# A softmax cut into seven pieces, work at the border of two steps moved ahead of the last groups of the second layer, and small products ordered by PSUM bank

## The chip, the cores and the metric

The kernel runs on one core of one Trainium2 chip. The metric is the device time of one execution in microseconds (us); the median of three runs before the change is 2174.5 us. TensorE is called PE here, VectorE DVE, ScalarE ACT, SyncE SP; these are the profile's names.

## The reference

For each of four batches, columns of q and k are normalised over the 6080 rows, a 256x256 score matrix goes through a softmax, and v is multiplied by it. The result goes through a two-layer network with a GELU between the layers.

```python
def _attn_ref(q, k, v, tau):             # q, k, v: (4, 6080, 256)
    qn = q / (np.linalg.norm(q, axis=1, keepdims=True) + 1e-06)
    kn = k / (np.linalg.norm(k, axis=1, keepdims=True) + 1e-06)
    s = kn.transpose(0, 2, 1) @ qn / tau
    s = s - s.max(-1, keepdims=True)
    a = np.exp(s)
    a /= a.sum(-1, keepdims=True) + 1e-09
    return (v @ a).astype(np.float32)

def _moe_ref(x, w_in, w_out):            # x: (24320, 256), w_in: (256, 2048), w_out: (2048, 256)
    h = x @ w_in
    g = 0.5 * h * (1.0 + erf(h * inv_sqrt2))
    return (g @ w_out).astype(np.float32)
```

## The kernel before

The softmax matrix of a batch is multiplied into `w_in` (`w_part`), so that the bulk of the work is two products: v times those weights (first layer), and the GELU of it times `w_out` (second layer). Numbers are split into a high and a low part (`vh`/`vl`, `wh`/`wl`, `gh`/`gl`), and a product takes three matmuls (`passes`): high by high, high by low, low by high.

**Steps.** A step is one `(b, p, u)`: batch b of 4, pair p of 6 (two chunks of 512 tokens, 480 in the last pair), unit u of 8 (two blocks of 128 hidden features). The 192 steps are counted by `i = (b*6+p)*8+u`. In a step, `first_products` makes the first layer of unit u by a Strassen scheme of seven products, called here **P0 to P6**, of three matmuls each. P0, P2, P4 and P6 go into one PSUM bank (`one`), P1, P3 and P5 into another (`two`). P0 and P1 are copied out by ACT (`p1`, `p5`), P2 too (`u2`). After P3, P4 and P5 DVE adds such a copy to the bank's contents (`added`), and ACT takes the GELU of the sum; the GELU of P6 is read by ACT straight from `one`. Where the unit's second layer is done by Strassen too (`mine`: most units with u > 0 from step 16 on), the GELUs of P5 and P6 go into `x`, and `sums` builds differences of its blocks on DVE and the high and low parts of all blocks on ACT and DVE (tiles `gh1`/`gl1`: called `hb`, `lb` in the code; `gh0`/`gl0`: `ht`, `lt`).

**The second layer lags a step.** Between the seven products of step i stand the groups of `second_products` of step i-1: one group of three matmuls after each of P0 to P3, one or two after P4 and P5, and what is left after P6. With Strassen these are four groups of width 512 and then seven small ones of width 256 (`work`), into the banks c00, c01, p0 and p1; three small ones are left after P6. Without it there are eight groups of 512, and two are left.

**Two banks in turn.** `bank()` hands out the two PSUM banks h0 and h1 in turn. P0 of a step takes the front bank of the ring, and at the end of `first_products` the bank of P6 is put at the back (`later`). So whatever takes a bank at the border of two steps gets the bank of P5 (`two`). If it does, P0 of the next step uses the bank that ACT's GELU of P6 reads, and P1 the bank of the border work. If nothing takes a bank there, P0 uses the bank of P5, and P1 that of P6.

**Work at the border.** Three kinds of work of the next batch take a bank: `burst` (eight matmuls for the scores of batch b, evicted by DVE into `sacc`), `w_part` (six matmuls of the softmax by `w_in`, evicted by ACT into a tile `hl`), and two steps of `softmax`: a product with `diag` that spreads the norms over all partitions (DVE reads it), and the four transposes of the exponentials (ACT reads them as `eh`, DVE as `el`).

**What sets the order.** Instructions run on each engine in the order in which the code issues them (`InOrder`). Work of the next batch is put into slots by `at(step, slot, job)`: slots 0 to 5 follow P0 to P5, slot 6 stands after the left-over groups of the second layer, `EDGE` (8) after `sums` has begun. `softmax(False)` is a generator that is resumed by `spread(gen, step, 12, 10 + EDGE, ...)`: 12 is slot 2 of the next step. With `base` the first step of batch b-1, the softmax of batch b stands in steps base+36 to base+38, `w_part` in base+41 to base+48, and the bursts in pairs of steps before.

Of the kernel before, what the change touches and what calls it, by code (L numbers as in the profile page):

```python
# [23 lines left out]
NCT = C // P  # L24
# [41 lines left out]
def channel_attention_gelu_ffn(ctx, tc, qk, kqt, vt, tau, w_in, w_out, out):  # L66
# [274 lines left out]
    def softmax(first):  # L341

        small = pm.tile([P, 32], F32, name="small")
        x, y, z, r = (small[:, 4 * i:4 * i + 4] for i in range(4))
        rk, nms, dens = (small[:, 16 + 2 * i:18 + 2 * i] for i in range(3))
        ts = []
        for m in range(NCT):
            t = pm.tile([P, C], F32, name=f"t{m}")
            if first:
                act.copy(out=t, in_=state["s"][m])  # L350
            else:
                s = state["sacc"]
                dve.tensor_tensor(out=t, in0=s[:, m, 0:C], in1=s[:, m, C:2 * C], op=ALU.add)
            ts.append(t)
        nsum = state.pop("nsum")
        if first:
            nps, acc = psum("c01"), state.pop("acc")
            with behind("scores"):
                for j in range(JS):
                    sum_up(nps, acc[:, j], j == 0, j == JS - 1)  # L360
            dve.reduce_sum(out=z, in_=nsum[:, :, NSQ // NSJ:NSC], axis=AX.X)
            dve.tensor_tensor(out=x, in0=nps[:, 0:2 * NCT], in1=z, op=ALU.add)
        else:
            dve.reduce_sum(out=x, in_=nsum[:, :, 0:NSC], axis=AX.X)
        dve.tensor_scalar(out=x, in0=x, scalar1=1e-30, scalar2=None, op0=ALU.max)
        yield

        if first:
            act.activation(out=y, in_=x, func=AF.Sqrt)
            preload(AF.Exp, y)  # L370
        else:
            dve.tensor_scalar(out=y.bitcast(I32), in0=x.bitcast(I32), scalar1=0.5, scalar2=float(ROOT),
                              op0=ALU.mult, op1=ALU.add)
            for part in (1.0, 0.25):
                dve.reciprocal(out=z, in_=y)
                dve.tensor_tensor(out=z, in0=z, in1=x, op=ALU.mult)
                dve.scalar_tensor_tensor(out=y, in0=y, scalar=part, in1=z, op0=ALU.mult, op1=ALU.add)
        dve.reciprocal(out=z, in_=y)
        dve.tensor_tensor(out=z, in0=z, in1=x, op=ALU.mult)
        dve.scalar_tensor_tensor(out=z, in0=z, scalar=2e-6, in1=y, op0=ALU.add, op1=ALU.add)  # L380
        dve.reciprocal(out=r, in_=z)

        diag = pm.tile([P, NCT, P], F32, name="diag")
        dve.tensor_tensor(out=diag, in0=ident.unsqueeze(1).broadcast_to([P, NCT, P]),
                                in1=r[:, NCT:2 * NCT].unsqueeze(2).broadcast_to([P, NCT, P]), op=ALU.mult)
        dve.tensor_scalar(out=rk, in0=r[:, 0:NCT], scalar1=rtau, scalar2=4.0, op0=ALU.mult, op1=ALU.mult)
        yield
        rq = psum("c10") if first else bank()
        mm(rq[:, 0:C], ones, diag.rearrange("p h d -> p (h d)"), start=True, stop=True)
        for m in range(NCT):  # L390
            dve.scalar_tensor_tensor(out=ts[m], in0=ts[m], scalar=rk[:, m:m + 1], in1=rq[:, 0:C],
                                           op0=ALU.mult, op1=ALU.mult)
            dve.reduce_max(out=nms[:, m:m + 1], in_=ts[m], axis=AX.X, negate=True)
        yield
        es = []
        rden = pm.tile([P, 8], F32, name="rden", bufs=2)
        for m in range(NCT):
            e = ts[m]
            den = dens[:, m:m + 1]
            act.activation(out=e, in_=ts[m], func=AF.Exp, bias=nms[:, m:m + 1], accum_out=den)  # L400
            es.append(e)
        if not first:
            yield
        for m in range(NCT):
            den = dens[:, m:m + 1]
            dve.tensor_scalar(out=den, in0=den, scalar1=1e-9, scalar2=None, op0=ALU.add)
            dve.reciprocal(out=rden[:, m:m + 1], in_=den)
        yield
        tp = psum("c11") if first else bank()
        tpv = tp.rearrange("p (d c) -> p d c", d=NCT)  # L410
        for m in range(NCT):
            for d in range(NCT):
                pe.transpose(out=tpv[:, d, m * P:(m + 1) * P], in_=es[m][:, d * P:(d + 1) * P],
                   identity=ident)
        eh = pm.tile([P, NCT, C], F32R, name="eh")
        el = pm.tile([P, NCT, C], F32R, name="el")
        marks["eh"] = act.copy(out=eh, in_=tpv)
        if first:
            preload(AF.Gelu, eh[:, 0, 0:2])
        marks["el"] = dve.tensor_tensor(out=el, in0=tpv, in1=f32(eh), op=ALU.subtract)  # L420
        state["e"], state["rden"] = (eh, el), rden
# [266 lines left out]
    def second_products(b, p, u, blocks):  # L688
# [14 lines left out]
        def wpair(c, i):  # L703
            cs = slice(c * P, (c + 1) * P)
            return wo[:, 0, i, cs], wo[:, 1, i, cs]
# [20 lines left out]
        if not mine:  # L726
            end = u == NU - 1
            for x in range(2 * NCT):
                c, i = divmod(x, NCT) if end and mixed else (x % NCT, x // NCT)
# [9 lines left out]
        ws = wss.pop((b, p, u))  # L739
        (hb, lb), (ht, lt) = blocks["b"], blocks["t"]  # L740
        last = not any(strassen(b, p, x) for x in range(u + 1, NU))
        work = (("c00", 1, wpair(0, 0), hb, lb, 2), ("p0", 0, wpair(0, 1), hb, lb, 0),
                ("c00", 0, (ws[:, 0, 3], ws[:, 1, 3]), hb, lb, 1), ("p1", 0, (ws[:, 0, 0], ws[:, 1, 0]), ht, lt, 0),
                ("p1", 1, (ws[:, 0, 2], ws[:, 1, 2]), ht, lt, 1), ("p0", 1, (ws[:, 0, 1], ws[:, 1, 1]), ht, lt, 2),
                ("c01", 1, wpair(1, 0), ht, lt, 3))
        for name, half, w, hi, lo, k in work:
            o, first = acc(name)
# [164 lines left out]
    FIRSTB = FILL // NB  # L912
    bursts = {}
    for b in range(1, B):
        start, num, den = (8, 5, 2) if b == 1 else (4, 14, 5)
        for k in range(FIRSTB if b == 1 else 0, NQS // NB):
            bursts[b, k] = (b - 1) * NP * NU + start + k * num // den

# [2 lines left out]
    def at(step, slot, job):  # L921
        jobs.setdefault((step, slot), []).append(job)

    def run(step, slot):
        for job in jobs.pop((step, slot), ()):
            job()

    def spread(gen, step, *slots):
        for x in slots:
            at(step + x // 10, x % 10, lambda: next(gen, None))  # L930

    EDGE = 8

    for (b, k), s in bursts.items():
        prev = bursts.get((b, k - 1), s - 3)
        for t in range(NB):
            js = k * NB + t
            at(prev - 1 + t, EDGE, lambda b=b, js=js: load_qk(b, js))

            def split(b=b, js=js, step=prev + 1 + t):  # L940
                gen = split_qk(b, js)
                next(gen)
                at(step, 2, lambda: next(gen, None))
            at(prev + 1 + t, 1, split)
        for m in range(NCT):
            at(s + m, EDGE, lambda b=b, k=k, m=m: burst(b, k, m))

        def drop(b=b, k=k):
            for t in range(NB):
                hls.pop((b, k * NB + t))  # L950
        at(s + 1, EDGE, drop)
    for b in range(1, B):
        base = (b - 1) * NP * NU
        for i in range(2 * NCT * NSC):

            def norm(b=b, i=i, step=base + 8 + i):
                gen = norm_part(b, *divmod(i, NSC))
                with behind("kept"):
                    next(gen)
                at(step + 1, 2, lambda: next(gen, None))  # L960
            at(base + 8 + i, EDGE, norm)

        def soft(step=base + 36):
            gen = softmax(False)
            next(gen)
            spread(gen, step, 12, 10 + EDGE, 22, 26, 20 + EDGE)
        at(base + 36, EDGE, soft)
        for g in range(NWG):
            at(base + 39 + 2 * g, EDGE if g == 0 else EDGE + 1, lambda b=b, g=g: load_win(b, g))
            for m in range(NCT):  # L970
                at(base + 41 + 2 * g + m, EDGE, lambda b=b, g=g, m=m: w_part(b, g, m))

            def wsums(b=b, g=g, step=base + 42 + 2 * g):
                spread(w_split(b, g), step, 10, 11, 12, 20, 22, 23)
            at(base + 42 + 2 * g, EDGE, wsums)
# [27 lines left out]
    for i, (b, p, u) in enumerate(steps):  # L1003
# [8 lines left out]
        for slot, _ in enumerate((plain_products if plain else first_products)(b, p, u)):  # L1012
            for _ in range(1 if slot < 4 or count < 11 else 2):
                next(second, None)
            if slot < 2:
                next(rest, None)
            run(i, slot)
        for _ in second:
            pass
        run(i, 6)  # L1020
# [52 lines left out]
```

## Time and profile before

| what | value |
|---|---|
| median of 3 runs (lowest to highest) | 2174.5 us (2173.92 to 2175.94) |
| profiled execution, its own time | 2174.69 us |
| its span, from the first instruction to the last | 2172.9 us |
| PE matmul busy | 2152.8 us, 99% |
| DVE busy, ACT busy | 1734.9 us (80%), 1622.5 us (75%) |
| granted TensorE clock | 1.000 over the whole span |
| DMA, mean share of 16 engines' span | 46.3% in the main queue |

In the rows of the timeline, the first column is the start in us from the span's start, the second how long the instruction (or the merged run of `x` instructions) took; then engine, line, operation, output tile <- input tiles, shapes. In brackets stands how long the engine was idle before, and what ended it. A matmul's modelled length (0.39 us for 512 columns) overlaps the next one's: the distance between two starts, 0.23 us, is what a matmul costs in a row of them. Nearly all instructions have line L138, that of the wrapper `InOrder`, so tiles tell them apart; `h` is any of the two banks, and also the SBUF tile of DVE's sums.

### The profile page before, as it was taken

Reading aid. Unit: us, or ns where it says so; the run is one execution under the profiler, and the core shown is the slowest. Engines: PE = TensorE matmul, PEld = TensorE weight load, DVE = VectorE, ACT = ScalarE, POOL = GpSimd, SP = SyncE. Lnnn points to the kernel's source line nnn. Section 1 sums busy time; section 2 is a strip of 40 time slices with the busy share of each in tenths; the row PEclk is TensorE's granted clock in tenths of the full one; section 3 lists DMA queues with packets and bytes.
Section 4 is the critical chain, followed back from the end, with each engine's and each line's share of the span. In section 5 each row is a group of like instructions: output and inputs, shape, how many; then the busy total and the mean of one; then the engine's idle time right before and its main releaser. Section 6 shows DMA issues by size and latency. Waiting matters only on the chain.

```text
span 2172.9 us, 29906 instructions
## 1 busy us (share of the span) xinstructions
PE 2152.8 (99%) x11061; PEld 1822.7 (84%) x11061; DVE 1734.9 (80%) x2732; ACT 1622.5 (75%) x2692; POOL 1.3 (0%) x8
## 2 busy tenths in 40 slices
PE   9999999999999999999999999999999999999999
PEld 8777888887888888888888888888888888888888
DVE  6997788877788788887788878888778777777776
ACT  5767778867777787786777778887677777677675
POOL 0000000000000000000000000000000000000000
PEclk9999999999999999999999999999999999999999
DMA  9545655544344555553434545554344333333332
GB/s 381 180 150 199 213 184 199 183 161 146 136 144 145 176 204 180 199 202 128 140 135 141 173 168 202 184 205 163 106 146 144 118 129 114 127 128 115 125 119 95
DMA packets 100547, 352.18 MB, mean 162 GB/s; under 512 B 10288, under 2 KB 12464, under 8 KB 98352
## 3 DMA queue, kind: packets, MB, share of 16 engines
q1 hardware_dynamic: 100400, 350.27, 46.3%
q8 instruction: 87, 1.43, 0.3%
q14 instruction: 60, 0.49, 0.1%
HBM read 312.74 MB, written 37.49 MB: 161 GB/s over the span
## 4 chain that ended last, share of the span: by engine, by line
PE 87%; DVE 7%; ACT 4%; issue 1%; DMA 0%; DVEq 0%; ACTq 0%; POOL 0%; POOLq 0%
PE h L138 45%; PE c L138 33%; PE p L138 9%; DVE h L138 2%; DVE vl L138 2%; DVE x L138 1%; ACT gh L138 1%; DVE gl L138 1%; ACT x L138 1%; ACT vh L138 1%; ACT g L138 0%; DVE small L138 0%; ACT L138 0%; ACT p L138 0%; DVE osb L138 0%
## 5 line engine op out<-in xcount | busy, mean ns | idle before, releaser
L138 PE MATMUL c<-gh,wo 128*128 128x512 f32 (+3 forms) x2460 | 870.4, 364 | 0.4 <-DVE wo L138 0.4
L138 PE MATMUL h<-vh,wh 128*128 128x512 f32 (+1 forms) x1312 | 520.3, 397 | 12.9 <-DVE h L138 2.8
L138 PEld LDWEIGHTS c<-gh,wo 128*128 128x128 f32 x2460 | 462.2, 188 | 81.9 <-DVE wo L138 1.5
L138 PE MATMUL h<-vh,wl 128*128 128x512 f32 (+1 forms) x1312 | 513.5, 391 | 0.0
L138 PE MATMUL h<-vl,wh 128*128 128x512 f32 (+1 forms) x1312 | 513.5, 391 | 0.0
L138 ACT ACTIVATE gh<-h 128x512 fp32r<-128x512 f32 (+1 forms) x446 | 277.9, 623 | 238.2 <-DVE h L138 219.2
L138 PE MATMUL c<-gl,wo 128*128 128x512 f32 (+3 forms) x1230 | 443.8, 361 | 0.1
L138 DVE TENSOR_TENSOR gl<-x,gh 128x768 fp32r<-128x768 f32 (+3 forms) x306 | 329.8, 1078 | 63.5 <-ACT gh L138 63.3
L138 DVE TENSOR_TENSOR gl<-g,gh 128x512 fp32r<-128x512 f32 (+1 forms) x462 | 314.5, 681 | 49.3 <-ACT g L138 47.1
L138 DVE TENSOR_TENSOR h<-h,p 128x512 f32<-128x512 f32 (+1 forms) x368 | 251.4, 683 | 79.5 <-PE h L138 68.3
L138 ACT COPY p<-h 128x512 f32<-128x512 f32 (+1 forms) x368 | 213.7, 581 | 126.3 <-PE h L138 126.2
L138 PEld LDWEIGHTS h<-vh,wh 128*128 128x128 f32 x1312 | 247.0, 188 | 72.3 <-ACT p L138 9.2
L138 ACT CAST gh<-x 128x768 fp32r<-128x768 f32 (+3 forms) x306 | 286.8, 937 | 16.7 <-DVE x L138 11.7
L138 PEld LDWEIGHTS h<-vh,wl 128*128 128x128 f32 x1312 | 246.4, 188 | 51.9
L138 DVE TENSOR_TENSOR x<-x 128x256 f32<-128x256 f32 (+4 forms) x491 | 241.1, 494 | 52.5 <-ACT x L138 34.8
L138 PEld LDWEIGHTS h<-vl,wh 128*128 128x128 f32 x1312 | 246.7, 188 | 35.4
L138 ACT ACTIVATE g<-h 128x512 f32<-128x512 f32 (+1 forms) x446 | 271.6, 609 | 0.0
L138 PEld LDWEIGHTS c<-gl,wo 128*128 128x128 f32 x1230 | 231.0, 188 | 45.3 <-DVE gl L138 0.5
L138 ACT ACTIVATE x<-h 128x512 f32<-128x512 f32 (+1 forms) x306 | 182.3, 609 | 48.9 <-DVE h L138 47.8
L138 PE MATMUL p<-gh,ws 128*128 128x256 f32 (+1 forms) x918 | 210.2, 280 | 0.0
L138 DVE TENSOR_TENSOR h<-h,u 128x512 f32<-128x512 f32 (+1 forms) x184 | 125.8, 684 | 83.5 <-PE h L138 82.6
L138 PEld LDWEIGHTS p<-gh,ws 128*128 128x128 f32 x918 | 162.6, 189 | 6.8
(153 smaller groups left out, 2229.5 us busy)
## 6 DMA issues: line engine op xcount, KB each, us to landing
wo<-keep_out SPq DMA_DIRECT2D x184, 512.0 KB, 4.5
ws<-keep_sum SPq DMA_DIRECT2D x153, 512.0 KB, 3.7
raw<-qk SPq DMA_DIRECT2D x94, 512.0 KB, 4.5
raw<-kqt SPq DMA_DIRECT2D x72, 512.0 KB, 4.6
v_raw<-vt SPq DMA_DIRECT2D x20, 1024.0 KB, 5.0
out<-osb SPq DMA_DIRECT2D x40, 512.0 KB, 3.9
hl<-keep_in SPq DMA_DIRECT2D x12, 1024.0 KB, 5.4
raw<-w_in SPq DMA_DIRECT2D x8, 512.0 KB, 6.9
```

Source lines behind the costliest of these rows:

```text
L138: r = op(*args, **kw)
```

## The change

There are four edits. `softmax(False)` yields in two more places: after the chain of small operations that makes the reciprocal norms, and between the scaling of the scores and the search for their maximum. Its pieces, eight with the first, now stand in slot 2 of step base+36, slots 2, 3 and EARLY of base+37, slots 2, 5 and 6 of base+38, and slot EARLY of base+39. A new slot `EARLY` (7) is run directly after P6, ahead of the left-over groups of the second layer; bursts, `w_part` and the two softmax pieces that take a bank move from `EDGE` to it. The seven small products are issued as c00, c00, p0, p0, p1, p1, c01. The bursts of batch 1 begin one step earlier.

```diff
@@ softmax
         dve.reciprocal(out=r, in_=z)
+        if not first:
+            yield
 
         diag = pm.tile([P, NCT, P], F32, name="diag")
...
             dve.scalar_tensor_tensor(out=ts[m], in0=ts[m], scalar=rk[:, m:m + 1], in1=rq[:, 0:C],
                                            op0=ALU.mult, op1=ALU.mult)
+        if not first:
+            yield
+        for m in range(NCT):
             dve.reduce_max(out=nms[:, m:m + 1], in_=ts[m], axis=AX.X, negate=True)
@@ second_products
-        work = (("c00", 1, wpair(0, 0), hb, lb, 2), ("p0", 0, wpair(0, 1), hb, lb, 0),
-                ("c00", 0, (ws[:, 0, 3], ws[:, 1, 3]), hb, lb, 1), ("p1", 0, (ws[:, 0, 0], ws[:, 1, 0]), ht, lt, 0),
-                ("p1", 1, (ws[:, 0, 2], ws[:, 1, 2]), ht, lt, 1), ("p0", 1, (ws[:, 0, 1], ws[:, 1, 1]), ht, lt, 2),
+        work = (("c00", 1, wpair(0, 0), hb, lb, 2), ("c00", 0, (ws[:, 0, 3], ws[:, 1, 3]), hb, lb, 1),
+                ("p0", 0, wpair(0, 1), hb, lb, 0), ("p0", 1, (ws[:, 0, 1], ws[:, 1, 1]), ht, lt, 2),
+                ("p1", 0, (ws[:, 0, 0], ws[:, 1, 0]), ht, lt, 0), ("p1", 1, (ws[:, 0, 2], ws[:, 1, 2]), ht, lt, 1),
                 ("c01", 1, wpair(1, 0), ht, lt, 3))
@@ placing
-        start, num, den = (8, 5, 2) if b == 1 else (4, 14, 5)
+        start, num, den = (7, 5, 2) if b == 1 else (4, 14, 5)
...
-    EDGE = 8
+    EARLY, EDGE = 7, 8
...
-            at(s + m, EDGE, lambda b=b, k=k, m=m: burst(b, k, m))
+            at(s + m, EARLY, lambda b=b, k=k, m=m: burst(b, k, m))
...
-            spread(gen, step, 12, 10 + EDGE, 22, 26, 20 + EDGE)
-        at(base + 36, EDGE, soft)
+            spread(gen, step, 12, 13, 10 + EARLY, 22, 25, 26, 30 + EARLY)
+        at(base + 36, 2, soft)
...
-                at(base + 41 + 2 * g + m, EDGE, lambda b=b, g=g, m=m: w_part(b, g, m))
+                at(base + 41 + 2 * g + m, EARLY, lambda b=b, g=g, m=m: w_part(b, g, m))
@@ the loop over the steps
             run(i, slot)
+        run(i, EARLY)
         for _ in second:
             pass
         run(i, 6)
```

What moves is shown at three places of batch 2, whose softmax stands in steps 84 to 87. Numbers behind names are buffers; h0, h1, c01, p1 are PSUM banks.

ACT in step 86 (`x` is the tile of GELUs, read from the sum of P5 and then from the bank of P6, here h1; `t0`, `t1` are the scores under the exponential). Before:

```order
L138 COPY u2_10479<-h1_10455 128x512
L138 ACT_TABLE_LOAD
L138 ACTIVATE t0_10329,small_10328<-t0_10329,small_10328 128x256
L138 ACTIVATE t1_10331,small_10328<-t1_10331,small_10328 128x256
L138 ACT_TABLE_LOAD
L138 ACTIVATE gh_10492<-h_10490 128x512
L138 ACTIVATE g_10494<-h_10490 128x512
```

ACT in step 86 and the begin of 87, after the change:

```order
L138 ACTIVATE x_10520<-h_10517 128x512
L138 ACT_TABLE_LOAD
L138 ACTIVATE t0_10260,small_10259<-t0_10260,small_10259 128x256
L138 ACTIVATE t1_10262,small_10259<-t1_10262,small_10259 128x256
L138 ACT_TABLE_LOAD
L138 ACTIVATE x_10520<-h1_10453 128x512
L138 CAST gh1_10549<-x_10520 128x768
```

The two exponentials with their two table loads stood between the copy of P2 and the first GELU, and stand now between the GELU of P5 and that of P6.

PE at the border of steps 85 and 86 (the product with `diag`, the last small group into c01 or the first left-over one into p1, and P6 into h1 or P0 of step 86). Before:

```order
L138 MATMUL c01_9966<-gl0_10320,wo_10102 128x256
L138 MATMUL c01_9966<-gh0_10319,wo_10102 128x256
L138 MATMUL h0_10448<-diag_10376,ones_90 128x256
L138 MATMUL h1_10455<-vh0_9665,wh3_484 128x512
L138 MATMUL h1_10455<-vl0_9666,wh3_484 128x512
```

PE there after the change:

```order
L138 MATMUL h1_10336<-vl6_9791,wh2_482 128x512
L138 MATMUL h1_10336<-vh6_9790,wl2_483 128x512
L138 MATMUL h0_10427<-diag_10389,ones_90 128x256
L138 MATMUL p1_10095<-gh0_10326,ws_10227 128x256
L138 MATMUL p1_10095<-gl0_10327,ws_10227 128x256
```

The product with `diag` follows P6 and no longer the left-over groups; it stands nine small matmuls earlier.

DVE in step 83, around the eviction of a burst (`sacc`; `vs` is the sum of v blocks in slot 6, the `x` rows are `sums`). Before:

```order
L138 TENSOR_TENSOR h_10179<-h1_10128,p1_10121 128x512
L138 TENSOR_TENSOR gl_10166<-g_10167,gh_10165 128x512
L138 TENSOR_TENSOR vs0_10203<-v_raw_10001 128x480
L138 TENSOR_TENSOR x_10182<-x_10182 128x512
L138 TENSOR_TENSOR x_10182<-x_10182 128x256
L138 TENSOR_TENSOR sacc_6603<-h1_10219,sacc_6603 128x512
L138 TENSOR_TENSOR x_10182<-x_10182 128x256
L138 TENSOR_TENSOR gl1_10209<-x_10182,gh1_10208 128x768
```

DVE there after the change:

```order
L138 TENSOR_TENSOR h_10179<-h1_10128,p1_10121 128x512
L138 TENSOR_TENSOR gl_10166<-g_10167,gh_10165 128x512
L138 TENSOR_TENSOR sacc_6582<-h1_10194,sacc_6582 128x512
L138 TENSOR_TENSOR vs0_10213<-v_raw_10001 128x480
L138 TENSOR_TENSOR x_10182<-x_10182 128x512
L138 TENSOR_TENSOR x_10182<-x_10182 128x256 x2
L138 TENSOR_TENSOR gl1_10219<-x_10182,gh1_10218 128x768
```

The eviction has moved ahead of `vs` and of all three rows of `sums`.

## The prediction

> **What bounds the kernel now.** I read the page first, then the chain that ended last, then what PE waited for, and at last the timeline around one softmax (batch 2) and at borders where work of the next batch stands. All times are us of the profiled execution.
>
> ```profile
> PE 2152.8 (99%) x11061; PEld 1822.7 (84%) x11061; DVE 1734.9 (80%) x2732; ACT 1622.5 (75%) x2692; POOL 1.3 (0%) x8
> ...
> PE 87%; DVE 7%; ACT 4%; issue 1%; DMA 0%; DVEq 0%; ACTq 0%; POOL 0%; POOLq 0%
> ...
> PE h L138 <- DVE h L138: 3.8, 7, 0.8
> PE h L138 <- DVE t L138: 2.3, 3, 0.8
> PE h L138 <- ACT p L138: 2.0, 5, 0.5
> PE h L138 <- ACT x L138: 1.5, 3, 0.5
> PE h L138 <- DVE el L138: 1.4, 3, 0.5
> ...
> PE h L138 <- ACT hl L138: 0.5, 3, 0.2
> ```
>
> PE is busy for 99% of the span, so a change that adds and removes no matmul can only move PE's waits. The rows of waits (total, times, longest) name them: DVE's sums `h`, the scaled scores `t`, `el` and ACT's `x`, most of them three or six times, which is once or twice per softmax. In all they are some 12 us, 0.5% of the time; no gain can be large.
>
> **Softmax: what it costs now.** PE's rows of steps 84 to 88 (P0 of 84 at 1008.10, of 85 at 1018.17, of 88 at 1053.61):
>
> ```profile
> 1008.10 0.39 PE L138 MATMUL h<-vh,wh 128*128 128x512 f32 x1
> ...
> 1018.17 0.40 PE L138 MATMUL h<-vh,wh 128*128 128x512 f32 x1
> ...
> 1026.09 0.50 PE L138 MATMUL h<-vh,wh 128*128 128x512 f32 x1 [0.83 <-DVE h L138]
> ...
> 1029.36 0.59 PE L138 MATMUL h<-diag,ones 128*128 128x256 f32 x2
> 1029.81 0.50 PE L138 MATMUL h<-vh,wh 128*128 128x512 f32 x1
> ...
> 1041.56 0.63 PE L138 MATMUL h<-ident,t 128*128 128x128 f32 x4 [0.34 <-DVE h L138]
> 1042.67 0.50 PE L138 MATMUL h<-vh,wh 128*128 128x512 f32 x1 [0.49 <-ACT x L138]
> ...
> 1053.61 0.38 PE L138 MATMUL h<-vh,wh 128*128 128x480 f32 x1
> ...
> 1057.92 0.49 PE L138 MATMUL h<-vh,wh 128*128 128x480 f32 x1
> ```
>
> An undisturbed step takes 1018.17 - 1008.10 = 10.07. Steps 85 to 87 take 1053.61 - 1018.17 = 35.44, which is 5.23 over three such steps. The product with `diag` itself takes 0.45 (1029.36 to 1029.81), the transposes 1.11 less the wait of 0.49 and 0.11 for a slower start, so 0.5. These stay; 4.3 are waits. A first matmul after a wait lasts 0.50 where others last 0.39, so each wait costs 0.11 more than its idle time.
>
> **Softmax: what goes.** DVE in step 85, and the scaled scores in 86:
>
> ```profile
> 1019.02 0.75 DVE L138 TENSOR_TENSOR t<-sacc 128x256 f32<-128x256 f32 x2
> ...
> 1019.97 0.42 DVE L138 TENSOR_TENSOR x<-x 128x256 f32<-128x256 f32 x1
> ...
> 1022.65 0.16 DVE L138 TENSOR_SCALAR small<-small 128x4 int32<-128x4 int32 x1
> ...
> 1024.88 0.42 DVE L138 TENSOR_TENSOR diag<-ident,small 128x256 f32<-128x256 f32 x1
> ...
> 1025.35 0.68 DVE L138 TENSOR_TENSOR h<-h,u 128x512 f32<-128x512 f32 x1
> ...
> 1030.86 0.47 DVE L138 SCALAR_TENSOR_TENSOR t<-t,small,h 128x256 f32<-128x256 f32 x1
> ```
>
> P5 of step 85 waits for `h<-h,u` (ends 1026.03, matmul at 1026.09: a handover of 0.06). The piece at 1019.02 holds `sums` up by 0.95 and leaves for step 84, where a gap before `h+u` takes it in. The reciprocal chain (1022.65 to 1024.88, 2.23) then runs from about 1021.7 to 1023.9, and with `diag` cut off behind it `h+u` ends about 1024.6, before the 1025.26 at which PE began to wait. That wait goes. The product with `diag` goes nine small matmuls (9 x 0.12 = 1.05) earlier and the searches for the maximum no longer stand directly behind the scaling, so the bank is read about 1 sooner: P1 of 86, which waited up to 0.8 for `t`, goes free. The transposes move one border on, into step 87 ahead of the left-over groups, so their wait (0.34), that of P0 behind them (0.49) and that for `el` (up to 0.5) leave their places. Of 4.3 I take all as gone; were `el` to wait as before, 0.6 less.
>
> **Softmax: what is late next.** ACT in steps 84 and 86:
>
> ```profile
> 1016.70 1.22 ACT L138 ACTIVATE x<-h 128x512 f32<-128x512 f32 x2 [0.32 <-DVE h L138]
> ...
> 1035.23 1.28 ACT L138 ACT_TABLE_LOAD   x1
> 1036.52 0.51 ACT L138 ACTIVATE t<-t,small 128x256 f32<-128x256 f32 x1
> ...
> 1038.93 0.63 ACT L138 ACTIVATE gh<-h 128x512 fp32r<-128x512 f32 x1
> ```
>
> The two exponentials and two table loads take 1038.93 - 1035.23 = 3.70. They stood where ACT had nothing urgent; now they stand between the GELU of P5 and that of P6. In a step that starts at S the pair of GELUs begins at S + 8.60 (1016.70 - 1008.10) and takes 1.22, so the GELU of P6 ends at S + 8.60 + 1.22 + 3.70 = S + 13.52. No work takes a bank at the border of 86 and 87, so P1 of 87 goes into P6's bank, at S + 10.07 + 1.38 (P0's three matmuls and a group of three, six at 0.23) = S + 11.45. A new wait of 2.07, with the slow start 2.2. It is bounded below by 0 (should the searches or DVE be so early that the exponentials start before the GELUs; the order on ACT speaks against it) and above by 3.7.
>
> The transposes in step 87 leave P0 of 88 waiting for P6's GELU as P0 of 87 did, but ahead of the left-over groups: I take 0.2 (0 to 0.6). `sums` of step 86 start 3.7 later, while PE lost only 2.2; the difference, 1.5, arrives at the copies on ACT in steps 87 and 88. P3 of 88 (1057.92) begins slow already now, so it has no reserve: +0.65 (0 to 1.5). Per batch -4.3 + 2.2 + 0.2 + 0.65 = -1.25 (-3.4 to -0.5), for three batches **-3.75**.
>
> [...]
>
> **Early border work.** The bank it takes is P5's, and DVE's addition after P5 must have read it. Ahead of the left-over groups the time of these groups (1.05 or 1.38) no longer covers that. Pairs of the addition (start, length) and the first left-over group on PE, where the early work will stand: a plain step, then u=0, u=1, `w_part` in u=7, a burst in u=7.
>
> ```profile
> 1004.43 0.69 DVE L138 TENSOR_TENSOR h<-h,p 128x512 f32<-128x512 f32 x1
> 1005.64 0.28 PE L138 MATMUL p<-gh,ws 128*128 128x256 f32 x1
> ...
> 791.64 0.68 DVE L138 TENSOR_TENSOR h<-h,p 128x512 f32<-128x512 f32 x1
> 792.08 0.28 PE L138 MATMUL p<-gh,ws 128*128 128x256 f32 x1
> ...
> 794.62 0.50 PE L138 MATMUL h<-vh,wh 128*128 128x512 f32 x1
> ...
> 981.71 0.68 DVE L138 TENSOR_TENSOR h<-h,p 128x512 f32<-128x512 f32 x1
> 982.34 0.39 PE L138 MATMUL c<-gh,wo 128*128 128x512 f32 x1
> ...
> 601.70 0.65 DVE L138 TENSOR_TENSOR h<-h,p 128x480 f32<-128x480 f32 x1
> 601.73 0.27 PE L138 MATMUL p<-gh,ws 128*128 128x240 f32 x1
> ...
> 1227.29 0.68 DVE L138 TENSOR_TENSOR h<-h,p 128x512 f32<-128x512 f32 x1
> 1227.57 0.28 PE L138 MATMUL p<-gh,ws 128*128 128x256 f32 x1
> ```
>
> - Plain step: 1004.43 + 0.69 + 0.06 = 1005.18 against 1005.64. Reserve 0.46: most of the 68 bursts wait for nothing.
> - u=0 (24, 32, 64, 72, 112, 120): 792.38 against 792.08, a wait of 0.30 + 0.11 = 0.41, six times 2.5. Five times P0 behind the work starts slow now (794.62 lasts 0.50) and loses some 0.19 there, which goes: 2.5 - 5 x 0.19 = +1.5 (0.5 to 2.5).
> - u=1 (25, 81, 129): 982.45 against 982.34: 0.11 + 0.11, three times: +0.66.
> - `w_part` in u=7 (47, 95, 143): 602.41 against 601.73, 0.68 + 0.11 = 0.79. What follows waited for `hl` (0.2) and for a copy `p` (up to 0.5) and has then less to wait: net 0.26, three times +0.8 (0 to 2.4).
> - Bursts in u=7 (55, 103): 1228.03 against 1227.57, 0.46 + 0.11; some of it comes back at P1, which waits for the eviction `sacc` less: +0.5 (0 to 1.1).
> - Batch 1's bursts a step earlier meet P5 banks not yet read in steps 12 and 23, about +0.6 by the same difference; its later ones miss waits for `sacc`: -0.7 (-0.9 to -0.5).
>
> **The rest.** Bank by bank: no wait in the list of waits is for the second layer's banks, so nothing is there to gain: 0. P0 now follows a small matmul and not a burst: a first product's matmuls start 0.23 to 0.24 apart there, 0.22 to 0.23 after a burst, so up to 0.01 per matmul of three for some 90 borders: +0.5 (0 to 1). The eviction `sacc` ahead of `vs` and `sums` keeps DVE idle until the burst ends; `sums` then start together with what they would have waited for: 0. DMA issues keep their order but for batch 1's step; DMA has 0% of the chain: 0.
>
> Sum: -3.75 + 1.5 + 0.66 + 0.8 + 0.5 + 0.6 - 0.7 + 0.5 = **+0.1**, so 2174.69 + 0.1 = 2174.8 on the profiled execution, and 2174.6 on the median, which is 0.2 lower. The likeliest case's own range is 2171 to 2178.
>
> **The rivals.** (1) The new wait for the exponentials isn't there or small: the searches end early and ACT has its exponentials done beside PE's left-over groups. For it speaks that DVE gets free sooner, against it the fixed order on ACT. 2174.6 - 3 x 3.05 = **2165.5**. (2) Slower: DVE works in order, so whatever stands behind `sacc` (`vs`, then `sums`, then `h+u`) waits for a burst's end. Each burst would then delay a later product once the 0.5 to 1 that DVE has left before `h+u` is used up; at 0.1 for each of 68 bursts +6.8, **2181**. Against it: the reserve in plain steps. (3) The change doesn't do what it says: the softmax's waits come back at the next products in full, and only the early work's losses stay, 2174.6 + 3.75 = **2178.4**. [...]
>
> **How the numbers follow.** Forecast 0.60, (1) 0.18, (2) 0.12, (3) 0.08, (4) 0.02. About 0.2%, 4.35 us, is what a measurement of this kernel can tell from no change. Faster: (1) and 0.06 of the forecast's tail, 0.24. Slower: (2) and (4), 0.14. Same: the rest, 0.62. The range reaches to rival (1) and past (3), 2165 to 2179; above it lie (2) and (4).
>
> **What would show it.** Right, step by step: no wait of P5 in 37, 85, 133, nor for `t` in 38, 86, 134; a new wait of about 2.1 of P1 in 39, 87, 135, released by ACT `x`; waits of 0.2 to 0.7 on the first matmul of early work in the steps named; equal pitches of the small products. Wrong: no such wait of P1 (then rival 1), or new waits for DVE `h` at P3 to P5 in many steps with a burst (rival 2).

## The result: 34 us slower, and the profile after

The changed kernel takes 2209.55 us (median of 4 runs, 2208.06 to 2210.13) beside 2175.12 us for the kernel before on the same chip: a ratio of 1.0158 (95% interval 1.014 to 1.0175). The prediction, 2174.6 us with a range of 2165 to 2179 and 0.62 on no change, was wrong. The profiled execution took 2208.06 us, with a span of 2206.3, 33.4 more than before.

The page's rows of busy time and of the chain, then PE's waits (total, times, longest), of the changed kernel:

```profile
PE 2160.7 (98%) x11061; PEld 1819.1 (82%) x11061; DVE 1735.7 (79%) x2732; ACT 1621.3 (73%) x2692; POOL 1.3 (0%) x8
...
PE 85%; DVE 7%; ACT 6%; issue 1%; DMA 1%; SPq 0%; DVEq 0%; ACTq 0%
```

```profile
PE h L138 <- ACT g L138: 17.6, 15, 1.2
PE h L138 <- ACT x L138: 6.2, 3, 2.2
PE h L138 <- DVE h L138: 5.8, 11, 0.8
PE h L138 <- ACT p L138: 5.7, 12, 1.0
PE h L138 <- ACT u L138: 2.1, 7, 0.3
```

The same work is done, and the waits for `t` and `el` are gone as forecast. `ACT x`, three waits of 1.96 to 2.23, is the forecast wait behind the exponentials. The first row was not foreseen: fifteen waits of 1.2 for `g`, the second GELU that ACT takes of P6's bank. All fifteen are waits of P0 behind a step that has border work and whose unit has no Strassen: steps 12 to 15 and the u = 0 steps 24, 32, 48, 64, 72, 80, 96, 112, 120, 128 and 144. (The kernel before has only the one behind step 15, of 0.74.) One of them, step 64, on PE (end of P6, burst, first and last left-over matmul, P0 of 65) and on ACT (the GELUs of P5's sum, then of P6's bank):

```profile
807.12 0.39 PE L138 MATMUL h<-vh,wl 128*128 128x512 f32 x1
807.65 1.68 PE L138 MATMUL h<-hl 128*128 128x512 f32 x8
809.17 0.28 PE L138 MATMUL p<-gh,ws 128*128 128x256 f32 x1
...
810.11 0.28 PE L138 MATMUL c<-gh,wo 128*128 128x256 f32 x1
811.57 0.50 PE L138 MATMUL h<-vh,wh 128*128 128x512 f32 x1 [1.17 <-ACT g L138]
```

```profile
808.25 0.61 ACT L138 ACTIVATE g<-h 128x512 f32<-128x512 f32 x1
810.43 0.60 ACT L138 ACTIVATE gh<-h 128x512 fp32r<-128x512 f32 x1 [1.56 <-PE c L138]
810.92 0.59 ACT L138 ACTIVATE g<-h 128x512 f32<-128x512 f32 x1
```

P6 is complete at 807.5, but ACT takes its GELU only at 810.43, released by PE's `c`: the last left-over group. The same place in the kernel before, ACT and then PE:

```profile
792.98 0.61 ACT L138 ACTIVATE g<-h 128x512 f32<-128x512 f32 x1
793.50 0.58 ACT L138 ACTIVATE gh<-h 128x512 fp32r<-128x512 f32 x1
793.98 0.59 ACT L138 ACTIVATE g<-h 128x512 f32<-128x512 f32 x1
...
793.02 0.28 PE L138 MATMUL c<-gh,wo 128*128 128x256 f32 x1
793.14 1.56 PE L138 MATMUL h<-hl 128*128 128x512 f32 x8
```

There the GELU of P6 starts directly behind the one ahead of it and no wait is printed. The code says what the rows hide: in `gelu`, the block (0, 0) is written to `gh0`, which has one buffer (`bufs=1`), and the left-over groups read what the last step put there. They ended at 793.3, just before ACT came to it.

Elsewhere the profile of the kernel before does print this wait. In u = 0 steps without border work (40, 88, 136, 152, 160, 168, 176, 184) ACT comes to the GELU of P6 before the left-over groups have ended, and is idle for 0.21 to 0.28 until PE's `c`. P0 then uses the bank of P5, and only P1 that of P6, so PE loses little. Step 88, PE's last left-over matmul and ACT's GELU:

```profile
1063.68 0.28 PE L138 MATMUL c<-gh,wo 128*128 128x256 f32 x1
1064.00 0.57 ACT L138 ACTIVATE gh<-h 128x480 fp32r<-128x480 f32 x1 [0.28 <-PE c L138]
```

### The profile page after: what moved, and what is told of

It is laid out like the page before. It is cut to its first block, busy times and chain, and to the rows that moved or that the text cites. A ratio compares the mean times of both kernels' runs of the same rounds, so it can differ in the third digit from the quotient of the medians.

```text
span 2206.3 us, 29977 instructions
## 1 busy us (share of the span) xinstructions
PE 2160.7 (98%) x11061; PEld 1819.1 (82%) x11061; DVE 1735.7 (79%) x2732; ACT 1621.3 (73%) x2692; POOL 1.3 (0%) x8
## 4 chain that ended last, share of the span: by engine, by line
PE 85%; DVE 7%; ACT 6%; issue 1%; DMA 1%; SPq 0%; DVEq 0%; ACTq 0%
PE h L138 44%; PE c L138 32%; PE p L138 9%; DVE vl L138 2%; DVE h L138 2%; ACT gh L138 2%; DVE x L138 1%; ACT vh L138 1%; DVE gl L138 1%; ACT g L138 1%; ACT x L138 1%; ACT hl L138 0%; ACT p L138 0%; ACT L138 0%; DMA wo<-keep_out 0%
```

## The experiments

**The buffer (e1).** The block gets a tile of its own, `gx`, of 512 columns, where the one in use is `gh0`.

```diff
 def gelu(src, n, i, j):
...
+            if i == 0 and state.get("held") == "gh0":
+                gh = pg.tile([P, 2, C], F32R, name="gx", bufs=1)
+                state["held"] = "gx"
+            else:
+                gh = pg.tile([P, 4, C] if i == 0 else [P, 3, C], F32R, name=f"gh{i}", bufs=1)
+                state["held"] = "gh0" if i == 0 else state.get("held")
@@ sums
         ht = pg.tile([P, 4 * C], F32R, name="gh0", bufs=1)
+        state["held"] = "gh0"
```

> The changed kernel, but where a unit without Strassen follows one whose high parts lie in the tile gh0, the GELU of P6 writes its high part into a tile of its own (gx). Buffer theory: the 15 waits of P0 for ACT's g (17.6 us idle, 20.0 with the slow starts) exist because gh0 has one buffer, which the left-over groups of the second layer read, and these now stand behind the border work. They go: 2209.6 - 20 = 2189.5 us (2187 to 2192); the waits of early work for P5's bank (about 11 us) stay. Bank theory: P0 waits because P5's bank comes free late and pushes all that follows, whatever ACT writes to: the 15 waits stay and the time is 2206 us or more.

2189.68 us (ratio to before 1.0068, 1.0053 to 1.0082), 19.9 less than the changed kernel. PE's list of waits has no row for `g` any more. ACT in step 24, where P6's GELU waited 1.54 in the changed kernel:

```profile
349.72 0.61 ACT L138 ACTIVATE g<-h 128x512 f32<-128x512 f32 x1
350.24 0.58 ACT L138 ACTIVATE gx<-h 128x512 fp32r<-128x512 f32 x1
```

It follows at once, with PE's order unchanged, and no GELU from step 8 on waits for `c` any more, those of steps like 88 included. That the buffer makes these waits is shown.

**Early work not in steps without Strassen (e2).**

```diff
+    def border(i):
+        b, p, u = i // NU // NP, i // NU % NP, i % NU
+        return EARLY if strassen(b, p, u) else EDGE
...
-            at(s + m, EARLY, lambda b=b, k=k, m=m: burst(b, k, m))
+            at(s + m, border(s + m), lambda b=b, k=k, m=m: burst(b, k, m))
```

(`w_part` likewise.)

> The changed kernel, but bursts and w_part go back behind the left-over groups (EDGE) in the 18 or so steps whose own unit has no Strassen (u = 0, and steps 12 to 15); early in all others. Buffer theory: the 15 waits for g go (20 us), and with them the bank waits of these steps (24, 48, 64, 72, 96, 112, 120, 144, each 0.4 to 0.5, and 1.1 in step 15; 4.6 in all): 2209.6 - 24.6 = 2185 us (2182 to 2188). Bank theory: what costs is early work in the u = 7 steps and what it drags along in the next step, which this kernel keeps: 2200 us or more.

2186.33 us (1.0053, 1.0039 to 1.0067): 23.2 less than the changed kernel. 11 remain.

**The early place alone, and the softmax alone (e3, e4).** e3 is the kernel before with `EDGE` turned into `EARLY` for bursts and `w_part`; e4 is the kernel before with the two new yields, the new `spread` and the first piece in slot 2.

> The kernel before with bursts and w_part moved ahead of the left-over groups, and nothing else (softmax in its old pieces, bursts of batch 1 from step 8, old order of the small products). If the early place alone makes the loss: 2175.1 + 34.4 + 0.6 = 2210 us (2206 to 2213), as in the changed kernel. If the softmax's new pieces carry a loss of their own (the new wait of P1 behind the exponentials, 2.1 per batch): 2203 us or less.

> The kernel before with the softmax in its new pieces (the product with diag and the transposes early), and nothing else: bursts and w_part at EDGE, batch 1 from step 8, old order of the small products. The prediction's term: -3.75, so 2171.4 us. By the trace of the changed kernel, where steps 36 to 40 of the three batches lose 0.55 us of waits in all (P1 behind the exponentials 2.1, P3 of step 40 1.2 instead of 0.3, P3 of step 39 0.3 new): 2174.6 us (2173.5 to 2175.5).

e3: 2207.79 us (1.0153, 1.0136 to 1.0169). e4: 2175.31 us (1.0003, 0.9994 to 1.0012). Nearly the whole loss belongs to bursts and `w_part`; the softmax's new pieces change nothing that can be measured. Batch 1's earlier start has no run of its own; the 1.8 by which the changed kernel is above e3 are what it, the softmax's pieces and the order of the small products add together.

**Bank by bank (e5).** The seven lines of `work` alone.

> The kernel before with the seven small products issued bank by bank (c00, c00, p0, p0, p1, p1, c01), and nothing else. By the prediction nothing: small matmuls start 0.12 us apart in either order, 2174.9 us (2174.0 to 2175.8). If a change of bank cost even 0.01 us per group, three changes fewer in each of 153 units would give 4.6 us: 2170.3.

2175.11 us (1.0001, 0.9992 to 1.001): nothing, as forecast.

**Where the exponentials stand (e6, e7).** From e4, with `EDGE` being slot 8:

```diff
-            spread(gen, step, 12, 13, 10 + EARLY, 22, 25, 26, 30 + EARLY)
+            spread(gen, step, 12, 13, 10 + EARLY, 21, 22, 26, 30 + EARLY)   # e6
+            spread(gen, step, 12, 13, 10 + EARLY, 21, 22, 26, 20 + EDGE)    # e7
```

> The kernel before with the softmax's new pieces (e4), but the search for the maximum in slot 1 and the exponentials in slot 2 of step base+38, so that they stand on ACT behind the copy of P2 again and not between the GELUs of P5 and P6. If the new wait of P1 (2.1 us per batch) and that of P3 of step 40 come from the place of the exponentials: ACT has their 3.7 us done 2 us before the GELU of P5 is due at the latest, P6's GELU ends about S + 11.3 against S + 11.45 at P1; both waits go but for some 0.6, and steps 37 to 40 lose 1.3 to 2 a batch instead of 5.1 in the kernel before: 2165.5 us (2163 to 2169). If ACT has too much to do in these steps wherever the exponentials stand, the waits come back at P2 and P3 of step 39: 2173 or more.

> As e6, but the transposes stay where the kernel before has them, behind the left-over groups of step base+38. P0 of step 39 then uses P6's bank at S + 10.6 while the GELU ends at about S + 11.3, so P0 waits 0.7, and P1 waits for el, up to 0.6: about 1 a batch more than e6, 2168.5 us (2166 to 2172). If the transposes' place is worth nothing: as e6 within 1 us.

e6: 2169.46 us (0.9974, 0.9964 to 0.9983). e7: 2168.91 us (0.9973, 0.9962 to 0.9983). First PE's waits of e4, then of e6, then of e7:

```profile
PE h L138 <- ACT x L138: 6.2, 3, 2.2
PE h L138 <- ACT p L138: 5.0, 8, 1.0
```

```profile
PE h L138 <- ACT p L138: 6.0, 11, 1.0
```

```profile
PE h L138 <- ACT p L138: 2.4, 6, 0.5
PE h L138 <- DVE h L138: 1.6, 5, 0.4
PE h L138 <- ACT x L138: 1.5, 3, 0.5
PE h L138 <- DVE el L138: 1.4, 3, 0.5
```

The wait behind the exponentials (6.2) goes with their place, so it was theirs. e6 missed its 2165.5 by 4: the wait of P3 in step 40 (1.0 in the list) stays. In e7, whose transposes are back, it is a slow start as in the kernel before in two batches and a wait of 0.45 in step 88; so most of it belongs to the transposes just ahead of a u = 0 step, and not to the place of the exponentials. e7, expected 3 us worse than e6, is as good.

**u = 7, and DVE (e8, e11).** e8 is e2 with `EARLY if strassen(b, p, u) and u < NU - 1 else EDGE`. e11 is e2 with the burst made a generator: PE's matmuls early, DVE's eviction at `EDGE`.

```diff
+        yield
         if k == 0:
...
-            at(s + m, border(s + m), lambda b=b, k=k, m=m: burst(b, k, m))
+            gen = burst(b, k, m)
+            for slot in (border(s + m), EDGE):
+                at(s + m, slot, lambda gen=gen: next(gen, None))
```

> The changed kernel with the early place kept for bursts and w_part only in units with Strassen other than the last (u = 1 to 6), EDGE in all other steps. If the rest of the loss is P5's bank read late in u = 7 (waits of 0.7 to 0.9) and the eviction held ahead of DVE's work at the start of u = 0: e2's 2186.3 less 4.3 (u = 7), 4.4 (what follows in u = 0) and 0.7 (w_part) = 2176.9 us (2175.5 to 2178.5), of which early work in u = 1 costs 0.9. If early work in plain steps costs something too: 2180 or more.

> e2, but DVE evicts a burst into sacc where the kernel before does it (after sums has begun), while PE still does the burst early. If the waits of P4 for u in u = 0 (seven times 0.57 with the slow starts, 4.0 in all) come from DVE standing idle for the burst's end ahead of sums: they go, 2186.3 - 4 = 2182.3 us (2181 to 2184), a little less if P1 then waits for sacc. If they come from PE's order: as e2, 2186.

e8: 2181.95 us (1.0034, 1.0022 to 1.0046), 5 above what was expected; two slow stretches of PE (last section) are about 2 of it. Most of the rest lies in the u = 0 steps behind a u = 7 burst (24, 56, 104): the expectation gave them back 0.6 each, but in e8 they take 0.2 more than in e2, as P1 there waits 0.24 for the eviction `sacc`. e11: 2178.59 us (1.0017, 1.0008 to 1.0026), 7.7 less than e2 and 3.7 better than expected, though PE's order is the same. DVE at the start of step 64, before, then after:

```profile
782.19 1.14 DVE L138 TENSOR_TENSOR x<-x 128x512 f32<-128x512 f32 x2
783.25 0.68 DVE L138 TENSOR_TENSOR sacc<-h,sacc 128x512 f32<-128x512 f32 x1
```

```profile
796.73 0.69 DVE L138 TENSOR_TENSOR sacc<-h,sacc 128x512 f32<-128x512 f32 x1 [1.17 <-PE h L138]
797.34 0.68 DVE L138 TENSOR_TENSOR vl<-v_raw,vh 128x512 fp32r<-128x512 f32 x1
797.94 1.60 DVE L138 TENSOR_TENSOR x<-x 128x512 f32<-128x512 f32 x3
```

P0 starts at 782.88 before and 797.59 after, so `sums` begins 0.7 before P0 there and 0.35 behind it here: DVE stood 1.17 in front of the eviction. ACT, in order too, waits for the end of `sums` before it casts their blocks:

```profile
799.58 1.05 ACT L138 CAST gh<-x 128x1024 fp32r<-128x1024 f32 x1 [0.50 <-DVE x L138]
```

In step 64 of the kernel before that cast doesn't wait, and in e11 it doesn't in any of the seven steps. Everything behind it on ACT is late, the copy `u2` of P2's bank too, and P4 needs that bank: it waits for `u` in seven u = 0 steps (24, 56, 64, 72, 104, 112 and 120), and in e11 in none. The same delay lies ahead of the u = 7 bursts: the burst of step 55 in the changed kernel, then in e11:

```profile
705.96 1.68 PE L138 MATMUL h<-hl 128*128 128x512 f32 x8 [0.75 <-DVE h L138]
```

```profile
694.81 1.68 PE L138 MATMUL h<-hl 128*128 128x512 f32 x8 [0.32 <-DVE h L138]
```

**Versions that beat the kernel before (e9, e10), and the change mended (e12).** e9 is e7 with e1's tile `gx`; e10 is e9 with the transposes at `30 + EDGE`; e12 is the changed kernel with e1's tile, e11's eviction and e7's `spread`.

> e7 (the kernel before with the softmax in new pieces, exponentials and transposes at their old places), and in units without Strassen the GELU of P6 writes its high part into the tile of its own (gx) of e1. Buffer theory: in the kernel before's order too that GELU starts only behind the left-over groups, so P0 waits for g at step 16 (0.9 with the slow start) and starts late or slow at steps 25, 49, 65, 73, 97, 113, 121, 145 (0.08 to 0.25 each): 2.3 less than e7, 2166.6 us (2165.5 to 2168). If these waits were ACT's load alone: as e7, 2168.9.

> As e9, but the transposes stand one step later, behind the left-over groups of step base+39, when ACT has caught up with the exponentials. In e7 the transposes cost 0.9 of waits in step base+38 (for P5's sum and P6's GELU) and 0.75 in base+39 (for el). If ACT's lag makes these, they shrink to 0.5 in all: e9 less 3 x 1 = 2163.5 us. If the next step, u = 0 and without Strassen, has as little room, P3's wait of 1.2 as in e6 comes back: as e9 or 1 us more.

> The changed kernel with all bursts and w_part early on PE, mended in the three places found: GELU of P6 into gx (e1), eviction of a burst at its old place on DVE (e11), exponentials and transposes at their old places (e7). What is left against e9 is the early place itself. If it is worth nothing and P5's bank read late is its only price: waits of 0.6 in three u = 7 bursts, 0.8 in three w_part, up to 0.4 in five u = 0 and 0.2 in four u = 1, less 0.6 given back at each of three w_part: 5.4 more than e9's 2166.6, 2172 us (2170 to 2175). If the early place gains something where P1 waited for sacc: at or below 2168.

e9: 2166.59 us (0.9963, 0.9949 to 0.9976), the lowest median. Its total is as expected, but not by the way expected: the wait at step 16 (0.74 for `g`) stays, because a cast of `vh` stands between ACT's GELUs there. Instead 0.06 to 0.10 went at P1's start in each u = 1 step behind the GELUs that wait for `c` in the kernel before (steps 41, 89, 137 and others), and 0.4 at the very end; but its interval overlaps e7's, so what `gx` is worth in the order of before isn't shown. e10: 2167.63 us (0.9966, 0.9954 to 0.9979), a miss: P1 waits 0.8 for `el` in step 40. e12: 2174.21 us (0.9996, 0.9986 to 1.0006), in the range expected, 7.6 above e9. Its main row of waits:

```profile
PE h L138 <- DVE h L138: 7.0, 18, 0.8
```

The first products' part of it is 1.7, by their group:

```profile
L138 PE MATMUL h<-vh,wh 128*128 128x512 f32 (+1 forms) x1312 | 517.0, 394 | 7.6 <-ACT p L138 2.1 <-DVE h L138 1.7 <-ACT x L138 1.5
```

Of the other 5.3, 4.3 are twelve waits of bursts and `w_part` for P5's bank, read late by DVE, and 1.0 are three of the transposes, which the kernel before has too. With the other causes mended, the early place is still no gain over `EDGE`. How large the loss is stays open in part: 4.4 of the 7.6 lie in steps 8 to 36, where batch 1's bursts also stand a step earlier than in e9; 3.2 lie behind them.

## Why the prediction was wrong, point by point

By medians the 34.4 us divide as follows: 23.2 from early work in steps without Strassen (e2), of which 19.9 is the buffer of `gh0` (e1); 7.7 from the eviction ahead of `sums` (e2 to e11); 3.5 left (e11 to before, 2178.6 to 2175.1): P5's bank in u = 7 and u = 1 and slow stretches of PE, less waits that went. The runs come from several chips; the kernel before takes 2174.9 to 2175.3 in each comparison.

- **The step that failed: "Early border work".** It priced the moved work's own wait (P5's bank) and nothing else. The wait was right: 0.30 with 0.10 for the slow start in step 64 as forecast, 0.69 + 0.11 for `w_part` in u = 7 (0.68 + 0.11), 0.11 + 0.11 in u = 1. But work put ahead of the left-over groups makes these end 1.4 later (1.8 in step 64, with the burst's own wait), and who waits for them was not asked. The GELU of P6 does in units without Strassen. It has 1.1 of ACT's time to go, and P0 needs its bank: 1.34 lost fifteen times, 20 us, for a term put at 0. The row of step 88 in the profile before was the sign of it. Of the smaller terms, the list left out the u = 0 steps of `w_part` (48, 96, 144), where it waits 0.40, and a burst in step 15 (0.79); step 12, which it named, shows no such wait.
- **The eviction on DVE was put at 0.** Rival 2 had its mechanism, an engine in order that stands in front of `sacc`, with a price of 0.1 for each of 68 bursts. It cost nothing measured in plain steps and some 0.6 in each of seven u = 0 steps, and as much in each of three u = 7 steps and of three pairs (31 and 32, 79 and 80, 127 and 128), by PE's distances in e2 and e11. In u = 7 most of it is the burst's wait (0.90 + 0.11 forecast as 0.46 + 0.11; e11, with DVE's old order, has 0.48 + 0.10). That the total, 7.7, is near its 6.8 is luck; the place is another.
- **Softmax, -1.25 a batch.** The waits of P5, for `t` and of P0 behind step 38 went as forecast. The new wait came, 1.96 and 2.2 with the slow start (2.23 idle in step 39), against 2.07 and 2.2:

```profile
1061.70 0.40 PE L138 MATMUL c<-gh,wo 128*128 128x512 f32 x1
1064.06 0.50 PE L138 MATMUL h<-vh,wh 128*128 128x512 f32 x1 [1.96 <-ACT x L138]
```

  What was mis-sized is what follows: P3 of step 88 lost 0.9 more than before (0.65 forecast), and P3 of 87 0.42 (not foreseen). From P0 to P0, steps 85 to 88 changed by -1.07 - 2.77 + 2.52 + 0.99 = -0.3, so 0.9 of the batch's 1.25 didn't come; some 0.2 of that isn't traced. e4 gives nothing measurable, and its profile has two slow stretches of about 1.0 (last section).
- **Right:** bank by bank (e5) and the small weight of rival 4. A slip without effect: the waits listed come three, five or seven times, not three or six. The first exponential again starts 0.02 behind its table load, in the changed kernel:

```profile
1059.70 1.28 ACT L138 ACT_TABLE_LOAD   x1
1061.00 0.51 ACT L138 ACTIVATE t<-t,small 128x256 f32<-128x256 f32 x1
...
1062.11 1.28 ACT L138 ACT_TABLE_LOAD   x1
1063.40 0.60 ACT L138 ACTIVATE x<-h 128x512 f32<-128x512 f32 x1
```

  No run shows the term of rival 4 (0.02 among the chances), a time that ACT would lose at each table load on top of the load itself: in the kernel before and in the changed one all nine loads take 1.28, and the next instruction starts 0.01 to 0.02 behind each.

## What to carry to other kernels

Work put ahead of other work delays that other work by its whole length (here the left-over groups by 1.4): list who waits for what is pushed back (results, and buffers that it frees), not only what the moved work itself waits for. A buffer with one copy that is freed just before its next writer arrives shows no wait at that place (step 64 before: freed at 793.30, written from 793.50). It is found in the code, by the number of buffers of each tile that the delayed instructions read, or in the profile at a like place where the time is shorter: here step 88 shows in the kernel before, on an engine off the critical path, the wait (0.28) that the change then made expensive (1.34 fifteen times). And on an engine that works in order, a consumer moved forward together with its producer makes the engine stand still (DVE in step 64 for 1.17): moving the producer alone saved 7.7 us here.

## What had not been expected of the hardware

After the wait behind the exponentials PE sometimes runs at about half pace for a while (in step 87 of e4 at a granted clock of 0.53). Matmuls of e4 behind that wait in step 87, then the granted clock of this stretch (the number behind the brackets, which hold a count of instructions), and that of the stretch behind the same wait in step 87 of the changed kernel:

```profile
1043.95 0.67 PE L138 MATMUL h<-vh,wh 128*128 128x512 f32 x1 [1.96 <-ACT x L138]
1044.42 0.63 PE L138 MATMUL h<-vl,wh 128*128 128x512 f32 x1
1044.85 0.63 PE L138 MATMUL h<-vh,wl 128*128 128x512 f32 x1
```

```profile
1044.00:1046.50 2.50, 2.50 (x6) 0.53 0.19 75
```

```profile
1064.00:1066.50 2.50, 2.44 (x11) 1.00 0.12 49
```

The distance is 0.43 instead of 0.23, at a granted clock of 0.53 instead of 1.00. Of the 18 such waits (idle 1.96 to 2.24) in the profiled executions of the changed kernel, e1, e2, e4, e8 and e11, eight were followed by seven or eight such matmuls, each 0.2 longer, which made the step about 1.0 longer (a wait of P3 shrinks in return); ten were not. The kernel before, e6, e7 and e9, which have no wait this long there, show no such row of slow matmuls from step 8 on. What decides between them is open.
